# Contiguous parameter loads, one store of the conv output, and a new step order in an attention and state-space kernel

## The chip, the cores and the metric

The kernel runs on 1 core of one Trainium2 chip. The metric is device microseconds (us) of one execution. Below, the engines carry the names of the profile: PE (TensorE), DVE (VectorE), ACT (ScalarE), POOL (GpSimd), SP (SyncE). SP, ACT and POOL also issue DMA transfers, each to queues of its own.

Each run has a state: a run over 1.5% above the fastest of the same kernel counts as slow.

## The reference, cut to what matters

Two independent parts, whose results are concatenated. The change touches only part B, the state-space convolution of 640 channels with 192 states each, over 2048 positions.

```python
# Part A: attention in 32 heads of 20 over 8 keys, each 2 apart; x is 2048x640
qkv = x @ wqkv;  logits = q . k[pos - 2*w], w = 0..7;  o = softmax(logits) . v;  a = o @ wo

# Part B
dt    = exp(log_dt)[:, None]                     # 640 values, bf16
logdA = dt * (A_re + 1j*A_im);  dB = dt * (B_re + 1j*B_im);  Cc = C_re + 1j*C_im   # 640x192 each
K     = einsum("dn,dnl,dn->dl", Cc, exp(logdA*l), dB).real
y     = irfft(rfft(u, 2L) * rfft(K, 2L))[:L] + u * Dskip
return concatenate([a, y], -1)
```

## The kernel before: the parts that matter

The kernel records 1,785 steps and executes them in an explicit list `ORDER`. That list fixes the program order of every engine: a step that waits holds back everything behind it on its engine.

Part B starts with a chain. Six parameters and `log_dt` are loaded (tiles `nat`, `ldt`). They are then "flipped": PE multiplies them with an identity, or with a diagonal of dt, so that the states come to stand on partitions (`ps_tr` in PSUM). From the flips come `ta` and `wi` (log-magnitude and phase per step), from those the tables of sines and magnitudes, and from the flipped B and C the generator `Gt`. Only then can the tables be multiplied into the kernel K (`ps_k`), and only after K come the transforms, the inverse and the output.

```python
# log_dt: channel d = 160g + 32c + t goes to partition 32g + t, column c
def ld_dt():
    for g in range(4):
        ACTE.dma_start(out=ldt()[32*g:32*g+32, :], in_=lsrc[g])
# parameters: the same layout, so rows of 192 bf16 = 384 B
def ld_nat(a):                       # a: A_re, A_im, C_re, C_im, B_re, B_im
    src = (...)[a].rearrange("(g c t) n -> g t c n", g=4, c=NCH, t=32)
    for g in range(4):
        (SP, ACTE, PQ)[min(a, 2)].dma_start(out=nt()[32*g:32*g+32, h], in_=src[g])
# x: four transposing loads on SP
for q in range(4):
    SP.dma_start(out=xT()[:, :, 512*q:512*q+512], in_=A_x[0, 512*q:512*q+512, :], transpose=True)

# u: 8 stages of 4 loads (rows of 160 bf16 = 320 B), regrouped by a DVE copy, written back to DRAM
def ld_u(us=us, s=s):
    for g in range(4):
        PQ.dma_start(out=us()[32*g:32*g+32], in_=usrc[g, :, s])

# inverse(i): i//4 = 0 does chunks 0,1,2 and i//4 = 1 chunks 3,4, for position block q = i%4
for o in range(0, 16, per):
    ...                                                   # matmuls into ps
    if n == 3: ACTE.copy(out=ysb()[:, o:o+per], in_=ps()[:])
    else:      V.tensor_tensor(out=ud()[:, o:o+per], in0=ps()[:], in1=ud()[:, o:o+per], op=A.add)
if n == 3:     V.tensor_tensor(out=ud()[:], in0=ud()[:], in1=ysb()[:], op=A.add)
def store(h):                                             # 192-B rows (3 chunks) or 128-B rows (2 chunks)
    for g in (2*h, 2*h+1):
        (PQ if h else SP).dma_start(out=dst_b[g, :, s, 32*cs[0]:32*cs[-1]+32], in_=ud()[32*g:32*g+32]...)
```

The softmax here doesn't subtract the row's maximum and nothing guards it: scores larger than these inputs give would overflow.

## Time and profile before

| | before |
|---|---|
| time, median of 3 runs | 404.41 us (402.19 to 408.61) |
| span of the profiled run | 406.0 us |
| busy: DVE, PE, ACT | 77%, 74%, 70% |
| DVE busy in the first 50 us | 12.5 us |
| last DVE instruction ends | 398.6 us, 7.4 us before the span does |

The page of the kernel before, its busy times, the DVE and DMA rows (tenths of 40 equal slices of the span) and the count of DMA packets:

```profile
span 406.0 us, 14847 instructions
PE 300.9 (74%) x6407; PEld 198.6 (49%) x6420; DVE 312.5 (77%) x472; ACT 284.0 (70%) x610; POOL 90.1 (22%) x165
DVE  1041499895199997899999977999967986864992
DMA  8999987873458496994611847820345348989766
DMA packets 67325, 72.55 MB, mean 179 GB/s; under 512 B 31140, under 2 KB 57748, under 8 KB 66492
```

No engine is full on average. The DVE row shows where it is not: the first five slices (50 us) are at 0 to 4 tenths, while the DMA row is at 8 or 9. The table of stretches gives it in us. The columns are the stretch, its length, the busy time of each engine, the granted clock, the DMA share (the time of all packets over 16 engines; it can pass 1, as here) and GB/s:

```profile
0.00:50.00 50.00, 21.46 (x139) 10.95 (x142) 12.50 (x30) 19.36 (x55) 17.91 (x37) 1.00 1.14 146
50.00:100.00 50.00, 37.13 (x266) 16.29 (x270) 45.60 (x91) 46.89 (x95) 22.39 (x32) 0.90 0.73 212
```

DVE (third engine column) goes from 12.50 to 45.60 of 50 us. What does it wait for? The timeline of DVE before gives start, length and, in brackets, the idle time ahead of an instruction and who ended it:

```profile
20.62 0.69 DVE L378 TENSOR_SCALAR wk<-ps_tr 128x512 f32<-128x512 f32 x1 [10.60 <-PE ps_tr L359]
...
45.91 0.69 DVE L394 TENSOR_TENSOR pr<-ps_tr,cc 128x512 f32<-128x512 f32 x1 [10.79 <-PE ps_tr L359]
```

Both waits are for flips. PE's timeline says what the flips waited for:

```profile
19.49 0.26 PE L359 MATMUL ps_tr<-dg,nat 128*128 128x64 bf16 x2 [7.96 <-DMA nat<-in_B_A_im_dram]
...
42.63 2.32 PE L555 MATMUL ps_p<-xT,w 128*128 128x512 bf16 x5 [8.84 <-DMA xT<-in_A_x_dram]
44.74 0.31 PE L359 MATMUL ps_tr<-dg,nat 128*128 128x64 bf16 x2
```

The first flip (19.49) waited for A_im. The DMA records, which give the times of every packet, say what A_im waited for. The 640 two-byte pieces of `log_dt` ahead of it on ACT's queue were all done by 4.7 us. Of A_im's own 640 rows half were done by 5.3 us, but the last only at 18.6 us, and from 6.5 us on x's transposed packets were in flight beside them. B_im was late: POOL's timeline has the load behind it waiting for B_im until 38.45.

```profile
38.45 0.58 POOL L571 DMA_DIRECT2D us<-in_B_u_dram  x1 [11.72 <-DMA nat<-in_B_B_im_dram]
```

x's four transposing loads took 41.42 us to issue, as SP's timeline shows:

```profile
4.71 41.42 SPq L302 DMA_TRANSPOSE xT<-in_A_x_dram  x4
```

One more wait comes near the end. In the chain of waits (start, length, what) before, 15 us go to the load that feeds the inverse:

```profile
341.89 15.06 DMA zq<-Zdram
```

### The profile page before, as it was taken

What the parts mean: (1) busy time and instruction counts of PE and PEld (TensorE: products, weight loads), DVE (VectorE), ACT (ScalarE), POOL (GpSimd) and SP (SyncE); (2) the same over time, 40 slices, a digit from 0 to 9 for tenths busy, and PEclk for the clock granted to TensorE, in tenths of its full rate; (3) what the DMA queues carried; (4) which work ended last, traced back from release to release, by engine and by line L of the source; (5) the groups of instructions that cost most, each with busy time, mean ns of one, the idle gap of its engine ahead of it and who ended that gap; (6) DMA issues with size and microseconds to landing.
All of it is one profiled execution on the core that took longest, in us unless ns stands there. A gap on an engine that the chain in (4) does not pass through costs nothing. (4 is left out here: it accounts for less than half of the span.)

```text
span 406.0 us, 14847 instructions
## 1 busy us (share of the span) xinstructions
PE 300.9 (74%) x6407; PEld 198.6 (49%) x6420; DVE 312.5 (77%) x472; ACT 284.0 (70%) x610; POOL 90.1 (22%) x165
## 2 busy tenths in 40 slices
PE   3263769865997974348799998679947879888884
PEld 1121324323543463036586777459625656575673
DVE  1041499895199997899999977999967986864992
ACT  2371389999999798138989868698614718668952
POOL 8050256720000021404110013200020120222252
PEclk9999989996999975558979989898886989969998
DMA  8999987873458496994611847820345348989766
GB/s 130 119 196 110 177 218 215 256 249 121 133 173 253 167 297 160 262 283 130 157 54 37 281 122 197 251 83 3 123 123 158 108 139 291 384 251 282 199 123 135
DMA packets 67325, 72.55 MB, mean 179 GB/s; under 512 B 31140, under 2 KB 57748, under 8 KB 66492
## 3 DMA queue, kind: packets, MB, share of 16 engines
q1 hardware_dynamic: 57964, 54.41, 50.7%
q0 software_dynamic: 6576, 15.31, 15.4%
q10 hardware_dynamic: 2720, 1.89, 2.1%
q8 instruction: 50, 0.82, 0.8%
q14 instruction: 15, 0.12, 0.1%
HBM read 43.98 MB, written 24.98 MB: 170 GB/s over the span
## 5 line engine op out<-in xcount | busy, mean ns | idle before, releaser
L555 PE MATMUL ps_p<-xT,w 128*128 128x512 bf16 x287 | 75.6, 408 | 30.3 <-ACT st L558 16.9
L555 PEld LDWEIGHTS <-w 128*128 128x128 bf16 x300 | 29.6, 103 | 70.4 <-issue 28.3
L529 PE MATMUL ps_k<-Ytab,Xtab 128*20 128x33 bf16 (+1 forms) x2560 | 52.7, 246 | 12.6 <-issue 5.9
L529 PEld LDWEIGHTS <-Xtab 128*20 128x20 bf16 (+1 forms) x2560 | 44.9, 127 | 25.9 <-issue 22.2
L776 DVE TENSOR_TENSOR p<-vb,attn 128x2048 bf16<-128x2048 bf16 x40 | 47.6, 1217 | 9.9 <-PE ps_o L781 4.8
L618 ACT CAST A<-ps_f 128x512 bf16<-128x512 f32 x80 | 43.2, 608 | 13.9 <-PE ps_f L613 13.1
L720 DVE TENSOR_TENSOR prod<-qb,kb 128x2048 bf16<-128x2048 bf16 x40 | 47.6, 1218 | 3.9 <-PE ps_l L725 2.6
L769 POOL DMA_DIRECT2D vb<-vd x40 | 22.0, 556 | 122.0 <-DVE p L776 91.8
L672 ACT CAST S<-ps_f 128x512 bf16<-128x512 f32 x80 | 42.2, 621 | 4.5 <-PE ps_f L668 3.3
L558 ACT CAST st<-ps_p 128x512 bf16<-128x512 f32 x60 | 33.7, 585 | 15.9 <-PE ps_p L555 15.5
L668 PE MATMUL ps_f<-A,cT 128*64 128x128 bf16 x640 | 28.3, 222 | 6.2 <-ACT A L618 2.5
L725 PE MATMUL ps_l<-prod,cGs 128*32 128x512 bf16 x160 | 17.7, 454 | 15.9 <-DVE prod L720 15.7
L675 DVE TENSOR_TENSOR Yf<-S 128x1024 bf16<-128x1024 bf16 x40 | 25.7, 683 | 3.5 <-ACT S L672 3.4
L795 PE MATMUL ps_op<-wo,oT 128*128 128x320 bf16 x160 | 28.2, 325 | 0.1
L668 PEld LDWEIGHTS <-cT 128*64 128x64 bf16 x640 | 20.7, 109 | 14.6 <-issue 13.6
L571 POOL DMA_DIRECT2D us<-in_B_u_dram x32 | 20.0, 632 | 24.6 <-DMA nat<-in_B_B_im_dram 11.7
L189 DVE TENSOR_TENSOR krtmp<-Xtab,Xg 128x1536 bf16<-128x1536 bf16 (+2 forms) x30 | 20.5, 685 | 6.3 <-DMA Xg<-Gdram 6.1
L490 ACT ACTIVATE Stab<-ta 128x192 bf16<-128x192 f32 x80 | 23.7, 362 | 0.3 <-DVE Ytab L512 0.2
L695 ACT CAST Z<-ps_ia 128x512 bf16<-128x512 f32 x40 | 21.4, 599 | 3.5 <-PE ps_ia L689 3.3
L613 PE MATMUL ps_f<-cBD,U 128*64 128x128 bf16 x320 | 22.6, 300 | 0.4 <-ACT A L618 0.2
L689 PE MATMUL ps_ia<-cEA,Yf 64*128 64x128 bf16 x640 | 21.5, 221 | 1.3 <-ACT A L618 0.8
L613 PEld LDWEIGHTS <-U 128*64 128x64 bf16 x320 | 20.2, 205 | 3.7 <-issue 2.5
(104 smaller groups left out, 552.0 us busy)
## 6 DMA issues: line engine op xcount, KB each, us to landing
vb<-vd SPq DMA_DIRECT2D x40, 128.5 KB
vb<-vd POOLq DMA_DIRECT2D x40, 128.5 KB, 4.1
Gdram<-cs SPq DMA_DIRECT2D x22, 192.0 KB
HB<-k_HB SPq DMA_DIRECT2D x2, 2048.0 KB
Zdram<-Z SPq DMA_DIRECT2D x3, 1024.0 KB
zq<-Zdram SPq DMA_DIRECT2D x12, 256.0 KB
kb<-kd SPq DMA_DIRECT2D x4, 657.5 KB
us<-in_B_u_dram POOLq DMA_DIRECT2D x32, 80.0 KB, 4.8
```

The source lines that it names most:

```text
L490: st(lambda k=k: ACTE.activation(out=Stab[c]()[:, k - 1], in_=ta()[:, CW * c:CW * c + CW], func=ACT.Exp, scale=float(-16 * k)))
L529: MM(ps()[32 * g:32 * g + 20, i, :], lhsT=X[c]()[rows, part % 2, :, col + t0 + i], rhs=Y[c]()[rows, :, part % 2, col + t0 + i], start=(par ...
L555: MM(ps()[:], lhsT=w()[:, kt, 128 * ct:128 * ct + 128], rhs=xT()[:, kt, 512 * sc:512 * sc + 512], start=(kt == 0), stop=(kt == 4))
L558: st(lambda so=so, sc=sc, ps=ps: ACTE.copy(out=so()[:, sc], in_=ps()[:]))
L613: MM(ps()[64 * r:64 * r + 64, jj], lhsT=src(16 * dd + 4 * jq + jj), rhs=BD1()[:, r, :], start=(jj == 0), stop=True, skip_group_check=True, ...
L618: st(lambda o=o, ps=ps: ACTE.copy(out=A1[c]()[:, :, sig, o:o + 16].rearrange("p k (j g) -> p k j g", g=4), in_=ps()[:].rearrange("p j (k g ...
L668: MM(ps()[64 * dd:64 * dd + 64, kk, r], lhsT=T()[:, k, r, :], rhs=A1[c]()[:, k, :, 64 * dd:64 * dd + 64], start=(kk == 0 and r == 0), stop ...
L672: st(lambda h=h, ps=ps, Sp=Sp: ACTE.copy(out=Sp()[:, :, :, :, 2 * h:2 * h + 2, :].rearrange("p r s j k g -> p (r s) j k g"), in_=ps()[:].r ...
L675: st(lambda b=b, i=i, Sp=Sp: V.tensor_tensor(out=Yf[c]()[:, 2 * i:2 * i + 2, :, 32 * b:32 * b + 32], in0=Sp()[:, :, 1].rearrange("p r j k ...
L720: st(lambda pr=pr, ct=ct, u2=u2: V.tensor_tensor(out=pr()[:], in0=q()[:, ct].unsqueeze(1).to_broadcast([128, 4, PB]), in1=windows(k()[:, c ...
L776: st(lambda p2=p2, u2=u2: V.tensor_tensor(out=p2()[:], in0=v()[:, :, 2 * u2:2 * u2 + PB], in1=attn[b]()[:, u2].unsqueeze(1).to_broadcast([ ...
L795: MM(ps()[:], lhsT=oT[b]()[:, t, 128 * x:128 * x + 128], rhs=wo_sb()[:, t, 320 * eh:320 * eh + 320], start=(t == 0), stop=(t == 4))
```

## The change

The intent: load every parameter as one contiguous run per partition (channel d = 5p + c on partition p, so 1,920 B per partition instead of five rows of 384 B), load u likewise, and let the flips and the evictions from PSUM do the regrouping. Keep the `u*D` tiles until all five chunks have been added, and store each row of 320 B once. Give all steps a new order. The core of the diff, with the `ORDER` list and some regrouping views left out:

```diff
-    def ld_dt():
-        for g in range(4):
-            ACTE.dma_start(out=ldt()[32 * g:32 * g + 32, :], in_=lsrc[g])
-    st(ld_dt)
+    st(lambda: ACTE.dma_start(out=ldt()[:], in_=B_log_dt.rearrange("(p c) -> p c", c=NCH)))
     def ld_nat(a):
-        src = (...)[a].rearrange("(g c t) n -> g t c n", g=4, c=NCH, t=32)
-        for g in range(4):
-            (SP, ACTE, PQ)[min(a, 2)].dma_start(out=nt()[32 * g:32 * g + 32, h], in_=src[g])
+        src = (...)[a].rearrange("(p c) n -> p (c n)", c=NCH)
+        (SP, ACTE, SP, ACTE, SP, ACTE)[a].dma_start(out=nt()[:, h].rearrange("p c n -> p (c n)"), in_=src)
@@ flip: chunk c is now the innermost index of the PSUM tile @@
-        psb = [bank([128, 512], "ps_tr", tag) for _ in range(2)]
+        psb = [bank([128, 3, 32, NCH], "ps_tr", tag) for _ in range(2)]
...
+    def by_k(ap):
+        return ap.rearrange("p (k c t) -> p k c t", k=3, c=NCH)
+    def by_chunk(t, s):
+        return t.rearrange("p (c k t) -> p k c t", c=NCH, k=6)[:, s.start // 160:s.start // 160 + 3]
-        st(lambda s=s, ps=ps: ACTE.copy(out=ta()[:, s], in_=ps()))
+        st(lambda s=s, ps=ps: ACTE.copy(out=by_chunk(ta()[:], s), in_=by_k(ps())))
...
@@ u: two loads of 10,240 B per partition @@
-            for g in range(4):
-                PQ.dma_start(out=us()[32 * g:32 * g + 32], in_=usrc[g, :, s])
+        PQ.dma_start(out=us()[:]..., in_=B_u[0].rearrange("(l1 a h b) ch -> h (l1 a) (b ch)", a=4, h=2, b=8)[h])
@@ inverse: u*D for all chunks ahead; the store after the second add, 8 rows at a time @@
+        def store(o, h):
+            for g in (2 * h, 2 * h + 1):
+                (PQ if h else SP).dma_start(out=dst_b[g, :, 16*q+o:16*q+o+per], in_=ud[q]()[32*g:32*g+32, o:o+per])
...
-        for h in range(2):
-            st(lambda h=h: store(h))
```

## The prediction

> **What bounds the kernel now.** Over the span (406.0 us) no engine is full: VectorE is busy 312.5 us, TensorE 300.9, ScalarE 284.0 (busy table). The table of stretches splits it. In the first 50 us VectorE is busy only 12.5 us, ScalarE 19.4 and TensorE 21.5, while the DMA engines are at their limit (DMA share 0.8 to 1.3). From 60 us on VectorE is busy 15 to 20 of every 20 us, except 100 to 120 us, where ScalarE (19.9) and TensorE (19.3) are full. So: a start bound by loads, then three nearly full engines, VectorE first.
>
> The waits of the start are for loads that this change touches: TensorE waits 8.0 us for A_im, landing at about 19.5 us behind 640 two-byte packets of log_dt on its queue; VectorE waits 10.6 us for that flip and 10.8 us for the B_im flip, which runs only at 44.7 us (timeline). GpSimd, which issues B and u, is stuck 10.1 and 11.7 us behind its own loads. The Trainium skill ("DMA: Bandwidth & Descriptors", Specifications) says transfers under 512 B miss line rate; this trace has 31,140 of 67,325 packets under 512 B.
>
> **What the change does.**
> - Parameters: 24 loads in 384-B rows become 6 with 1,920 B per partition, issued by ScalarE and SyncE ahead of weights and x, none by GpSimd. log_dt: 640 two-byte pieces become 128 of 10 B. Regrouping moves into the flips: 20 matmuls each as before, evictions of the same size (0.5 to 0.7 us), only strided.
> - u: 32 loads of 320-B rows (20.0 us of GpSimd) become 2 with 10 KB per partition; the eight regroup copies (0.81 us each) stay.
> - conv output: 320-B rows once instead of 192 + 128 B: half the packets (16,384 to 8,192), same 32 issues, all after the last chunk. The u*D products become 4 of about 1.5 us instead of 6.3 us in all: nothing.
> - Order: summed from the trace's durations, work per engine stays (VectorE about -2, ScalarE -5 us: four activation-table loads fewer). The z loads of the inverse stage now stand before the 4 MB of HB, not behind; they are 15.06 us of the chain of waits.
>
> **How much lies on the path.** I expect the six parameters to have landed by 10 to 15 us and the generator (G) work to start near 12 to 18 us rather than 46. VectorE had done about 9 us of work by 46 us, so it could gain up to 27 us. ScalarE, saturated from 60 to 120 us, had done 17 us by then and limits the gain to about 20. x (10,240 transposed 256-B packets) is not faster by itself and the first projections still come at 25 to 40 us, but the new order puts 45 ScalarE operations ahead of the first projection eviction, so this should not bind. The inverse stage gives perhaps 5 us (VectorE idles 4.6 us in 340 to 360 us). The tail stays about 7 us: last add, GpSimd's issues of 0.65 us, a landing of about 4 us.
>
> 404.4 - 20 - 5 gives about 379; I say 377 us, range 364 to 391. Chances: faster 0.89, within 2% 0.09, slower 0.02.
>
> **What would show it.** First B_im flip before 20 us; VectorE over 30 us busy in the first 50 us; no wait of TensorE on A_im over 3 us; packets under 512 B down by some 18,000; no 15-us wait for z; VectorE's total within 4 us of 312.
>
> **What would make it wrong.** Parameters still delayed by x's transposes and the 1.3 MB halves of u; projections so late that attention starves the end; strided PSUM evictions much slower; a lower TensorE clock (now 0.89 mean, 0.5 at 160 to 180 us) when work is denser; stores bunched at the end stretching the tail.

## The result

| | before | after |
|---|---|---|
| time, median (all runs) | 405.29 us (402.19 to 408.61, 4 runs) | 385.33 us (383.80 to 389.74, 4 runs) |
| ratio of fast runs, 95% interval | | 0.9519 (0.943 to 0.9609) |
| span profiled, mean granted clock | 406.0 us, 0.887 | 384.3 us, 0.884 |
| DVE busy in the first 50 us | 12.5 us | 34.15 us |
| last DVE instruction ends, then to the end | 398.6 us, 7.4 us | 372.75 us, 11.5 us |

A ratio is the mean time of one kernel's fast runs over that of the other kernel's fast runs of the same rounds, so it is not quite the ratio of the medians quoted beside it. The kernel is faster by 4.8%. A later control of five rounds on another chip (the run after_again, below) gave 386.67 us.

The same lines of the page after:

```profile
span 384.3 us, 14774 instructions
PE 306.9 (80%) x6420; PEld 201.0 (52%) x6420; DVE 313.6 (82%) x468; ACT 277.6 (72%) x606; POOL 62.4 (16%) x119
DVE  2289996949898799999899999899998586389870
DMA  7972084782935374657986452578157579289957
DMA packets 60428, 72.54 MB, mean 189 GB/s; under 512 B 24372, under 2 KB 51364, under 8 KB 59340
```

DVE does the same work (313.6 against 312.5 us) in a shorter span. Its row is full from the fourth slice on. The first and second stretch of 50 us after:

```profile
0.00:50.00 50.00, 32.98 (x165) 16.42 (x166) 34.15 (x83) 34.41 (x89) 3.01 (x9) 0.90 0.61 173
50.00:100.00 50.00, 35.96 (x600) 18.47 (x600) 40.83 (x75) 33.54 (x70) 8.62 (x12) 0.77 0.63 196
```

In the first 50 us DVE has done 21.65 us more than before. In the second stretch it gave back 4.8. The two waits of 10 us have become shorter. DVE's timeline after:

```profile
8.64 0.66 DVE L380 TENSOR_SCALAR wk<-ps_tr 128x480 f32<-128x480 f32 x1 [2.88 <-PE ps_tr L355]
...
19.72 0.66 DVE L380 TENSOR_SCALAR wk<-ps_tr 128x480 f32<-128x480 f32 x1 [7.42 <-PE ps_tr L360]
...
24.52 1.15 DVE L400 TENSOR_TENSOR Gt<-pr 128x960 bf16<-128x960 f32 x1
```

The 7.42 us that are left are of another kind. PE's timeline after shows no wait for a parameter beyond the first and one of 0.91 us. From 4.75 to 23.5 us PE works through the flips almost without a pause, 0.4 us for each group of a 128x32 and two 64x64 matmuls. From some 10 us on the start is bound by PE.

```profile
4.75 0.24 PE L357 MATMUL ps_tr<-cident,nat 128*128 128x32 bf16 x1 [4.75 <-DMA nat<-in_B_C_re_dram]
...
9.50 2.02 PE L355 MATMUL ps_tr<-dg,nat 128*128 128x96 bf16 x10 [0.91 <-DMA nat<-in_B_A_re_dram]
```

The flips of B_im, the last two in PE's new order, start at 20.3 instead of 44.7 us. They now stand ahead of the first projection (23.18 us on PE), so they no longer wait for x. SP's timeline after has x's loads issued in 21.55 us, half of the time before, though x's loads themselves were not changed:

```profile
2.73 21.55 SPq L293 DMA_TRANSPOSE xT<-in_A_x_dram  x4
```

The 15-us wait for `zq` is gone from the chain of waits. Others have come in. The chain after has these transfers and "issue" (time in which the engine waited for nothing that the profile shows):

```profile
2.12 8.37 DMA nat<-in_B_B_re_dram
...
52.84 8.88 DMA Gdram<-cs
72.77 6.67 DMA Gdram<-cs
...
314.06 6.50 DMA K<-Kdram
323.45 3.81 issue
...
354.45 6.96 DMA vb<-vd
```

Its first line says that B_re had landed at 10.5 us (2.12 + 8.37). The later ones cost DVE its pace for a while: it is busy 13.14 us of 60 to 80 (18.52 before) and 9.65 us of 320 to 340 (15.44 before).

So the 21.7 us of the two spans split like this. DVE was 21.65 us of work ahead at 50 us, and its last instruction ends 25.8 us earlier. The tail after that instruction has grown by 4.1 us (25.8 - 4.1 = 21.7).

### The profile page after: what moved, and what is told of

Its sections match the earlier page's. It is cut to its first block, busy times and chain, and to the rows that moved or that the text cites. A ratio compares the mean times of both kernels' runs of the same rounds, so it can differ in the third digit from the quotient of the medians.

```text
span 384.3 us, 14774 instructions
## 1 busy us (share of the span) xinstructions
PE 306.9 (80%) x6420; PEld 201.0 (52%) x6420; DVE 313.6 (82%) x468; ACT 277.6 (72%) x606; POOL 62.4 (16%) x119
## 4 chain that ended last, share of the span: by engine, by line
PE 43%; DVE 16%; ACT 15%; DMA 11%; issue 10%; POOL 2%; SPq 1%; POOLq 0%; DVEq 0%; ACTq 0%
PE ps_k L531 9%; PE ps_p L557 8%; PE ps_f L611 7%; PE ps_op L793 4%; DMA Gdram<-cs 4%; DMA vb<-vd 3%; DVE p L774 3%; PE ps_f L666 3%; PE ps_l L723 2%; DMA nat<-in_B_B_re_dram 2%; ACT S L670 2%; PE ps_ia L687 2%; ACT A L616 2%; ACT Stab L492 2%; DMA K<-Kdram 2%
## 5 line engine op out<-in xcount | busy, mean ns | idle before, releaser
L557 PE MATMUL ps_p<-xT,w 128*128 128x512 bf16 x300 | 82.5, 436 | 22.1 <-ACT st L560 20.4
L557 PEld LDWEIGHTS <-w 128*128 128x128 bf16 x300 | 31.8, 109 | 68.6 <-issue 41.5
L616 ACT CAST A<-ps_f 128x512 bf16<-128x512 f32 x80 | 44.6, 618 | 20.8 <-PE ps_f L611 20.6
L767 POOL DMA_DIRECT2D vb<-vd x40 | 22.5, 567 | 137.5 <-DVE p L774 100.5
L666 PE MATMUL ps_f<-A,cT 128*64 128x128 bf16 x640 | 29.5, 234 | 2.5 <-ACT A L616 1.2
L666 PEld LDWEIGHTS <-cT 128*64 128x64 bf16 x640 | 22.1, 118 | 12.6 <-issue 10.5
L793 PE MATMUL ps_op<-wo,oT 128*128 128x320 bf16 x160 | 26.7, 306 | 0.2 <-issue 0.2
L492 ACT ACTIVATE Stab<-ta 128x192 bf16<-128x192 f32 x80 | 24.9, 370 | 0.0
L611 PE MATMUL ps_f<-cBD,K 128*64 128x128 bf16 x320 | 16.4, 250 | 8.1 <-issue 5.8
L611 PEld LDWEIGHTS <-U 128*64 128x64 bf16 x320 | 20.3, 204 | 4.9 <-issue 4.2
L188 DVE TENSOR_TENSOR Xtab<-Xtab,Xg 128x1536 bf16<-128x1536 bf16 (+2 forms) x30 | 20.6, 686 | 0.2
L687 PEld LDWEIGHTS <-Yf 64*128 64x128 bf16 x640 | 18.5, 94 | 4.3 <-issue 3.5
```

What stands on the lines that cost most here:

```text
L492: st(lambda k=k: ACTE.activation(out=Stab[c]()[:, k - 1], in_=ta()[:, CW * c:CW * c + CW], func=ACT.Exp, scale=float(-16 * k)))
L557: MM(ps()[:], lhsT=w()[:, kt, 128 * ct:128 * ct + 128], rhs=xT()[:, kt, 512 * sc:512 * sc + 512], start=(kt == 0), stop=(kt == 4))
L611: MM(ps()[64 * r:64 * r + 64, jj], lhsT=src(16 * dd + 4 * jq + jj), rhs=BD1()[:, r, :], start=(jj == 0), stop=True, skip_group_check=True, ...
L616: st(lambda o=o, ps=ps: ACTE.copy(out=A1[c]()[:, :, sig, o:o + 16].rearrange("p k (j g) -> p k j g", g=4), in_=ps()[:].rearrange("p j (k g ...
L666: MM(ps()[64 * dd:64 * dd + 64, kk, r], lhsT=T()[:, k, r, :], rhs=A1[c]()[:, k, :, 64 * dd:64 * dd + 64], start=(kk == 0 and r == 0), stop ...
L687: MM(ps[dd]()[:, jj].rearrange("p l r -> p (l r)"), lhsT=Yf[c]()[d, q, 4 * jq + jj, :], rhs=EA()[d, q, :], start=(jj == 0 and q == 0), sto ...
```

## The experiments

Two questions: which part of the change made the start faster, and by what; and what happened to the rest, that is, the order, the single store and u. All experiments gave the reference's results. One I could not build: the new structure under the old order, since the old list has no place for the new steps and my attempts ended in deadlock or ran out of on-chip space. Order and structure of the second half are therefore told apart only by what the experiments below leave over.

### params_only, params_queues, small_rows, u_old: which part carries the gain

Theory 1: fewer and larger packets in the parameter loads are the gain. Theory 2, the rival: it is the move of the loads to the front of the SP and ACT queues. These four ran on one chip with 7 runs of the kernel before (median 409.66 us).

params_only is the kernel before with contiguous loads of parameters and `log_dt` and the new flips, but the old queues, old u, old stores and the old order. (Eight steps that fill the second half of the phase table had to move ahead of their first reader.)

```diff
-            (SP, ACTE, PQ)[min(a, 2)].dma_start(out=nt()[32 * g:32 * g + 32, h], in_=src[g])
+        (SP, ACTE, PQ)[min(a, 2)].dma_start(out=nt()[:, h].rearrange("p c n -> p (c n)"), in_=src)
```

> The kernel before with the contiguous parameter rows and the regrouping flips alone; queues as before (A_re on SyncE, A_im on ScalarE, B and C on GpSimd), order as before but for eight steps (the second half of the phase table must now be ready before the first phase is used). Theory 1 (small rows and the 640 two-byte packets held the start): A_im lands before 9 us instead of 19.5, B_im before 15 us instead of 44.7, VectorE is over 20 us busy in the first 50 us (12.5 before), and the ratio to the kernel before is 0.95 to 0.975, that is 10 to 20 of the 20 us gained. Theory 2 (queues and order made the gain): A_im lands earlier but the ratio stays within 0.985 to 1.01.

Measured: 386.98 us median, ratio 0.9454 (0.9382 to 0.9526). This bundle (contiguous loads, the flips that they need, eight moved steps) has the whole gain of the change, a little more than theory 1 said (0.95 to 0.975). The first stretch of its table:

```profile
0.00:50.00 50.00, 38.62 (x210) 19.70 (x211) 33.91 (x74) 37.96 (x101) 23.38 (x43) 0.97 0.94 233
```

DVE's 33.91 us match the 34.15 of the changed kernel. Its last DVE instruction ends at 376.3 us (22.3 earlier than before), and the tail is 7.6 us, close to the 7.4 before.

params_queues puts these loads on the SP and ACT queues, as the change does.

```diff
-        (SP, ACTE, PQ)[min(a, 2)].dma_start(...)
+        (SP, ACTE, SP, ACTE, SP, ACTE)[a].dma_start(...)
```

> As the run before it, and the six parameter loads issued first, three from SyncE and three from ScalarE, ahead of x and the weights. Theory 1: at most 4 us better than the rows alone, ratio 0.945 to 0.97. Theory 2 (queue and place in the queue decide): clearly better than the rows alone, by over 6 us, and B_im's first flip before 20 us only here.

Measured: 388.69 us, 0.95 (0.9421 to 0.958). Not better than params_only: theory 2 falls.

small_rows is the changed kernel with each parameter loaded in five pieces of 384 B per partition.

```diff
-        (SP, ACTE, ...)[a].dma_start(out=nt()[:, h].rearrange("p c n -> p (c n)"), in_=src)
+        for c in range(NCH):
+            (SP, ACTE, ...)[a].dma_start(out=nt()[:, h, c], in_=src[:, CW * c:CW * c + CW])
```

> The changed kernel with each parameter loaded as five pieces in 384-byte rows on the same queues (30 issues instead of 6, 3840 packets instead of 768), all else as changed. Theory 1 (packet size): parameters land 5 us or more later than in the changed kernel (last first flip at 11 to 15 us there), and the time is 3 to 8 us longer, ratio to the kernel before 0.96 to 0.975. Theory 2 (order and queue): within 2 us of the changed kernel, ratio 0.947 to 0.957.

Measured: 394.62 us, 0.9601 (0.9512 to 0.9691); the last flip starts at 31.0 instead of 22.5 us, and DVE is busy 25.5 us in the first 50. So small rows cost, but not the whole gain: SP and ACT were held up by their own 15 issues each, so that x's transposes began only at 14.30 us, after the parameters.

u_old is the changed kernel with u loaded as before (the 32 loads and their stages put back).

```diff
-    st(lambda: ld_u(0))
...
+            for g in range(4):
+                PQ.dma_start(out=us()[32 * g:32 * g + 32], in_=usrc[g, :, s])
```

> The changed kernel with u loaded as before (32 GpSimd loads in 320-byte rows, small staging tiles, the first two right after the C flips, the others after the copy that frees their tile), order otherwise as changed. Theory 1 (u's rows are off the path): ratio 0.945 to 0.96, as the changed kernel, GpSimd busy about 80 us instead of 62. Theory 2 (u's two big early loads are part of the gain): over 5 us slower than the changed kernel, ratio over 0.965, VectorE waiting for u or for GpSimd in the first 80 us.

Measured: 385.83 us, 0.9409 (0.9343 to 0.9474). The loading of u is worth nothing that these runs show: the 28 us of POOL's busy time that the change saves (90.1 to 62.4) were not on the path.

### po_2b, po_small, po_both: which small packets

params_only removed two kinds of small packets, the 640 two-byte pieces of `log_dt` and the 384-B rows. These three put one or both back into params_only. They ran on one chip (kernel before: 409.29 us).

```diff
 po_2b
-    st(lambda: ACTE.dma_start(out=ldt()[:], in_=B_log_dt.rearrange("(p c) -> p c", c=NCH)))
+        for c in range(NCH):
+            ACTE.dma_start(out=ldt()[:, c:c + 1], in_=B_log_dt.rearrange("(p c) -> p c", c=NCH)[:, c:c + 1])
 po_small
-        (...)[min(a, 2)].dma_start(out=nt()[:, h].rearrange("p c n -> p (c n)"), in_=src)
+        for c in range(NCH):
+            (...)[min(a, 2)].dma_start(out=nt()[:, h, c], in_=src[:, CW * c:CW * c + CW])
 po_both: both
```

> The kernel with the contiguous parameter rows alone (ratio 0.945 to the kernel before), and log_dt loaded again in 640 two-byte pieces ahead of A_im on ScalarE's queue. Theory A (the two-byte pieces delayed A_im and with it the start, as the prediction says): A_im's flip moves from about 12 us to over 15 us and the ratio rises to 0.96 to 0.98. Theory B (the 384-byte rows and what they do to GpSimd's queue and to x's transposes): under 2 us change, ratio 0.935 to 0.955, A_im's flip within 2 us of 12 us.

> The kernel with the contiguous parameter rows alone, and each parameter loaded again in 384-byte pieces (five issues of 128 rows; A_re on SyncE, A_im on ScalarE, B and C on GpSimd as before). Theory B: B_im's flips over 10 us later than there (over 33 us instead of 21 to 26), x's 256-byte transposed packets take over 40 ns on average in the first 40 us (19 to 42 ns there, about 80 before), ratio 0.97 to 1.0. Theory A: ratio 0.94 to 0.955, B_im's flips within 4 us.

> Both of these undone: contiguous layout and regrouping flips kept, packets as small as in the kernel before. If packet size is the whole cause, the time is that of the kernel before: ratio 0.985 to 1.01. If the layout of the loads or the changed steps matter besides (fewer partitions per issue before, 4 issues of 32 partitions each), it stays under 0.97.

| | median us | ratio (95%) | `log_dt` there by | DVE busy in 50 us |
|---|---|---|---|---|
| params_only | 386.98 | 0.9454 (0.9382 to 0.9526) | 2.7 or before | 33.9 |
| po_2b | 404.63 | 0.9887 (0.9779 to 0.9994) | 28.1 | 12.15 |
| po_small | 396.08 | 0.9723 (0.9636 to 0.9811) | 5.7 or before | 29.3 |
| po_both | 394.33 | 0.9681 (0.9605 to 0.9757) | 7.2 or before | 25.3 |

1,280 bytes in two-byte pieces take away about four fifths of the gain in po_2b (0.9887 against 0.9454). But po_both, which has both kinds, is better than po_2b alone. At 0.9681 it falls into the second branch of its expectation (under 0.97): with packets as small as in the kernel before, more than half of the gain is still there. Packet size is not the whole cause. In the timelines of PE the first B_im flip comes at 24.20 us in params_only and at 26.08 us in po_both, against 44.74 before:

```profile
24.20 0.58 PE L351 MATMUL ps_tr<-dg,nat 128*128 128x96 bf16 x5
```

```profile
26.08 0.58 PE L356 MATMUL ps_tr<-dg,nat 128*128 128x96 bf16 x5
```

What keeps it early (five load issues over 128 partitions instead of four over 32, the new flips, or the eight moved steps) no run here tells apart. po_small has the ratio that theory B expected (0.9723), but not its path: its B_im flips come only 1.8 us later than in params_only (25.96), not over 10, and x's transposed packets took 29 ns on average, not over 40. Its later projections wait for x instead. And in po_2b something other than the count of packets decides. The timelines of ACT and SP in po_2b (a run of the slow state; its start is what counts here):

```profile
28.08 1.28 ACT L334 ACT_TABLE_LOAD   x1 [28.08 <-DMA ldt<-in_B_log_dt_dram]
...
1.64 38.66 SPq L299 DMA_TRANSPOSE xT<-in_A_x_dram  x4
...
34.00 0.66 DVE L380 TENSOR_SCALAR wk<-ps_tr 128x480 f32<-128x480 f32 x1 [3.27 <-PE ps_tr L355]
```

In po_2b SP began with x's transposes at 1.64 us, while ACT was still issuing `log_dt` (0.74 to 3.09 us). In po_both SP first had five pieces of A_re to issue, and the transposes began at 4.08. So a new theory, R: it is a race. Small packets that are in flight together with x's transposes starve. Between 3.5 and 11.5 us of po_2b the DMA records show 223 two-byte packets done beside 1,741 transposed packets of 256 B, 7.8 for each; the last two-byte packet ended at 27.3 us (in po_both at 4.6 us, before x's first packet at 5.6). The Trainium skill ("DMA: Bandwidth & Descriptors", Queues, rings and completion order) gives a possible reason: an engine "round-robins between the queue rows it has work for, at *packet* granularity", and drains a packet of typically 9 to 17 descriptors before it switches. A queue with 640 tiny pieces would then get the same turns as one with large work. The trace does not confirm this: equal turns of equal length would give about one for one, not 7.8, and the length of a turn is not in the records. So the mechanism stays open; what the next run tests is only that being in flight together is what costs.

### po_2b_late_x and before_late_x: the race tested by order alone

po_2b_late_x is po_2b, with SP's five loads of constants moved ahead of x's transposes. No packet is added or removed.

```diff
-ORDER: 0 1 2 6 3 9 4 5 14 13 26 ...              (9, 4, 5 ...: 9 is the first transpose of x)
+ORDER: 0 1 2 6 3 19 20 21 22 23 9 4 5 14 13 26 ...
```

> The kernel with contiguous parameter rows and two-byte log_dt (404.6 us, log_dt landed only at 28 us), with one thing changed: SyncE issues its five constant loads before x's transposed loads, so that these start about 2.3 us later (about 4 us instead of 1.6). Theory R (a race: many small packets get through only one per turn once x's transposed packets are in flight): log_dt lands before 8 us, VectorE is over 25 us busy in the first 50 us instead of 12, and the time goes back to 384 to 394 us, ratio 0.94 to 0.965. Theory S (the two-byte pieces are slow in themselves): log_dt still lands after 15 us and the ratio stays over 0.975.

Measured: 391.52 us, 0.9576 (0.9434 to 0.9718), against 0.9887 without the move. The same lines of its profile (slow too, so like po_2b's):

```profile
7.79 1.28 ACT L334 ACT_TABLE_LOAD   x1 [7.79 <-DMA ldt<-in_B_log_dt_dram]
...
7.62 21.76 SPq L299 DMA_TRANSPOSE xT<-in_A_x_dram  x4
...
13.71 0.66 DVE L380 TENSOR_SCALAR wk<-ps_tr 128x480 f32<-128x480 f32 x1 [3.27 <-PE ps_tr L355]
```

The two-byte pieces are all still there. With the transposes starting 6 us later (7.62 instead of 1.64; I had expected 2.3) they have landed by 7.8 us instead of 28.1. DVE is busy 32.1 us in the first 50. Theory R holds for po_2b: not the small packets as such, but small packets together with the transposes, made its start late. It does not follow that `log_dt` was late in the kernel before. There SP first had four issues of A_re, the transposes were issued at 4.71 us, and `log_dt` was done by 4.7. What was in flight together with the transposes there was A_im.

before_late_x is the kernel before with x's transposes issued after all parameter loads and two small stores (of `st`, to `kd` and `vd`); nothing else is changed.

```diff
-ORDER: 0 1 2 6 3 9 4 5 14 13 26 7 12 48 ...
+ORDER: 0 1 2 6 3 4 5 7 8 16 17 18 9 14 13 26 12 48 ...
```

> The kernel before, small rows and all, with only its order of loads changed: x's transposed loads are issued after all parameter loads and after the two halo stores, which wait for GpSimd to have issued B and C. Theory R (what was lost at the start was lost to the transposed loads of x getting in front of the small packets): A_im's flip before 13 us instead of 19.5, the first B_im flip before 25 us instead of 44.7, x's first matmul 5 to 10 us later at most, ratio 0.945 to 0.975. Theory S (the small rows are slow in themselves): B_im's flip after 30 us, ratio over 0.98.

Measured: 399.32 us, 0.9698 (0.948 to 0.9917, from two fast runs of four): about half of the gain, by order alone. A_im's last row is done at 7.7 instead of 18.6 us, and its flip is early (DVE's `wk` at 11.81 instead of 20.62 us). So theory R holds for A_im. But the second half of the start stays late, as PE's timeline shows (slow):

```profile
34.51 0.58 PE L555 MATMUL ps_p<-xT,w 128*128 128x512 bf16 x1 [19.65 <-DMA xT<-in_A_x_dram]
```

In the old order a projection stands ahead of B's flips on PE, so the whole chain now waits for x instead. DVE is busy only 15.7 us in the first 50. The expectation of a large gain was half right. Moving x back is no substitute for contiguous loads, unless the flips are moved as well.

Why is x itself slow in these runs? By the DMA records the median of x's 10,240 transposed packets took 18 ns in each of before, after, before_late_x and params_only. The means differ: 52.6, 20.3, 36.7 and 24.7 ns, by a few long packets (10.8% of them took over 100 ns before, 0.3% after). In the kernel after, POOL had no load in flight from 8.8 us until 31.9 us; in the kernel before its gathers ran from 2.8 to 40.1 us with gaps of at most 2.5 us; in params_only they had gaps of 5.3 and 2.6 us within x's time. This is a correlation in the records. I have not tested it by itself.

### after_again, store_16, store_split: the tail

Where did the tail of 11.5 us come from? T1: it is the number of store issues (32, each 0.57 to 0.65 us on POOL). T2: it is the bytes and rows that the DMA engines still have to write after the last chunk, since all rows now wait for it. These three ran on one chip in 5 rounds (kernel before: 408.84 us). after_again is the changed kernel, unchanged, as the control.

> The changed kernel again, as the control for the two runs beside it: ratio 0.94 to 0.96; last VectorE instruction to end of span 11 to 12 us.

Measured: 386.67 us (381.55 to 388.37), 0.9619 (0.9435 to 0.9802). Few of the kernel before's runs counted as fast in these rounds, so the interval is wide.

store_16 halves the issues: 16 rows at once, after the second add.

```diff
-            for g in (2 * h, 2 * h + 1):
-                (PQ if h else SP).dma_start(out=dst_b[g, :, 16*q+o:16*q+o+per], in_=ud[q]()[32*g:32*g+32, o:o+per])
+            for g in (2 * h, 2 * h + 1) if o else ():
+                (PQ if h else SP).dma_start(out=dst_b[g, :, s], in_=ud[q]()[32*g:32*g+32])
```

> The changed kernel with the conv output stored once per 16 rows instead of per 8: 16 issues instead of 32, each twice as big. Theory T1 (the tail is the issue of 10 GpSimd and 12 SyncE stores at about 0.6 us each after the last add): the tail shrinks from 11.5 us to 7 to 9 us and the time falls by 2.5 to 4.5 us, 0.6 to 1.2 per cent under the control. Theory T2 (the tail is the writing of the bytes): tail stays 11 to 12 us, no gain.

Measured: 387.52 us (380.82 to 389.92). There is no ratio, since all but one of its runs count as slow beside its own fastest. The last DVE instruction ends at 376.2 us (in a slow run), and the tail is 11.6 us. With half of the issues the tail is the same: T1 falls as a matter of their number. SP's time for them did not halve, since each issue took longer (9.17 us for 6, against 7.09 us for 10). That the DMA engines and not SP set the pace is read from their share of busy time, 0.92 to 0.99 in both kernels (stretches of 3 to 4 us) until 7 to 8 us into the tail; no run tests it.

store_split stores as the kernel before does (192-B rows after chunks 0 to 2, 128-B rows after 3 and 4) within the new order.

```diff
-                (PQ if h else SP).dma_start(out=dst_b[g, :, 16*q+o:16*q+o+per], in_=ud[q]()[32*g:32*g+32, o:o+per])
+                (PQ if h else SP).dma_start(out=dst_b[g, :, s, chs], in_=ud[q]()[32*g:32*g+32, :, chs])
...
+                store(1, 0); store(1, 1)        # in the step of the add of chunks 0 to 2
```

> The changed kernel with the conv output stored as in the kernel before, chunks 0 to 2 when their add is done and chunks 3 and 4 after theirs, 16 rows each: 16,384 packets of 192 and 128 bytes instead of 8,192 of 320. If the half number of packets is worth something, 2 us or more slower than the control; if only the bunching of the issues at the end matters, as fast as the control or up to 3 us faster, tail 8 to 11 us.

Measured: 395.56 us (392.48 to 397.69), 0.9892 (0.9777 to 1.0007). This is the first branch of the expectation (2 us or more slower), and far beyond it: 8.9 us slower than the control beside it, and the runs of the two do not overlap. DVE's timeline, the last lines of store_split and then of the changed kernel:

```profile
374.15 2.56 DVE L863 TENSOR_TENSOR ud<-ps_ib,ud 128x512 bf16<-128x512 f32 x4 [0.32 <-PE ps_ib L856]
376.74 0.96 DVE L868 TENSOR_TENSOR ud<-ud,ysb 128x1536 bf16<-128x1536 bf16 x1
```

```profile
369.20 2.56 DVE L863 TENSOR_TENSOR ud<-ps_ib,ud 128x512 bf16<-128x512 f32 x4 [0.32 <-PE ps_ib L856]
371.79 0.96 DVE L867 TENSOR_TENSOR ud<-ud,ysb 128x1536 bf16<-128x1536 bf16 x1
```

In both kernels the very last DVE step is the add of chunks 0 to 2: under the new order these finish last, next to the others. So a split store can write only a part ahead. Half of the output's 8,192 rows go by SP's queue. When the last DVE instruction had ended, it still had 2,593 of its 4,096 rows of 320 B to write in the changed kernel; with split stores 1,024 rows of 192 B and all 4,096 of 128 B; in the kernel before 2,048 of 128 B. A row took a mean of 23 ns there at 320 B, 15 at 192 B and 13 to 16 at 128 B. The time of all packets that started after that instruction, over 16 engines, against the tail:

| | packets, us | tail, us |
|---|---|---|
| before | 4.5 | 7.4 |
| after | 8.7 | 11.5 |
| store_16 | 8.9 | 11.6 |
| store_split | 10.7 | 13.7 |

The differences agree, and each tail is about 3 us longer than its packets' time, so T2 stands. This covers 2 of the 8.9 us. Why the last DVE instruction comes 5 us later with split stores stays open. In its profile DVE waits 7.80 us for `vb` at 365.1 us, which the changed kernel's does not, and the granted clock was lower too (0.834 against 0.884).

The profile of the changed kernel has several gaps of PE with the label "issue", 9 of at least 1 us (17.8 us in all) against 4 (6.9 us) before. Each of them, in both kernels, falls together with one packet of 16,384 B on the DMA queue that the page calls "instruction", which ended 1.3 to 1.7 us before PE went on. (There are 50 such packets in either run, most of them without a gap.) The 3.81 us in the chain above are one of them. In params_only there are 2 (5.0 us). That PE waits for its own instructions there is argued from this coincidence. No run tests it.

## Why the prediction was right or wrong

The time, 385.33 us, lies in the range of 364 to 391, and 8 us above the centre.

**What bounds the kernel.** Right: a start bound by loads. The contiguous loads with their flips (params_only) give the whole gain, 0.9454. The step "A_im ... behind 640 two-byte packets of log_dt" is not what held A_im: in the kernel before those pieces were done by 4.7 us, and A_im's last row only at 18.6. What the prediction did not see is the race with x's transposes. before_late_x shows it for A_im: with x issued later, and the two-byte pieces still ahead, A_im was done by 7.7 us. That the two-byte pieces can lose this race themselves is shown by po_2b, where x starts earlier than in the kernel before. The Trainium skill's line that the prediction drew on ("DMA: Bandwidth & Descriptors", Specifications: at least 512 B for line rate) agrees in direction: of the parameter rows done before 12 us a 384-B one took 22 ns in the median in the kernel before (27 in the mean), a 1,920-B one 79 in the kernel after, about 17 against 24 B per ns. But this factor of under two is not what cost 20 us: 640 rows at 27 ns are about 1 us on 16 engines.

**"x ... is not faster by itself".** Nothing in x's loads was changed, but they did become faster: their issues went from 41.42 to 21.55 us. And the wait of 10.8 us which the prediction put down to loads "that this change touches" was in part a wait for x: B_im's flip stood behind a projection that waited 8.84 us for it. In the changed kernel the new order puts the flips ahead of every projection; in params_only, in the old order, x itself came early enough (first projection at 17.05 us). The prediction named neither. The result was right because all went the same way.

**Size of the start.** Predicted 20 us, measured 21.65 us of DVE lead at 50 us. The reason given for 20 instead of 27, that ScalarE is full from 60 to 120 us, is not what the trace after shows: ACT is busy 43.5 of these 60 us (58.9 before). So the close match is partly luck. "VectorE over 30 us busy in the first 50 us" (34.15), "no wait of TensorE on A_im over 3 us" (none) and "VectorE's total within 4 us of 312" (313.6) held. "First B_im flip before 20 us" missed narrowly, at 20.3: the flips had become bound by PE itself, and B_im's stand last.

**"The inverse stage gives perhaps 5 us".** The 15-us wait for z is gone, as predicted. DVE's lead at its last instruction is 25.8 us, 4.2 more than at 50 us. So the sum of the two terms, 25, was met by 25.8. That is luck in part. The lead was not kept on the way: it stood at 17.5 us at 340, after the new waits for `Gdram` and `K`, and 8.3 us came after that instead of the 5 predicted. And params_only, whose chain still has a wait of 6.81 us for `zq`, has a lead of 22.3 us at its last DVE instruction.

**"The tail stays about 7 us".** This is the mis-sized term: 11.5 us. The prediction counted half the packets and the same issues, and noted "all after the last chunk" without costing it. After the last DVE instruction the DMA engines had 8.7 us of packets left instead of 4.5. "Stores bunched at the end stretching the tail" stood among the risks. This term of 4.1 us is most of the distance between the sum (379) and the result (385.3). The other 2 us are no more than the spread of runs: the spans of the two profiles differ by 21.7 us, the medians by 19 to 20.

**Packets under 512 B "down by some 18,000".** Wrong: down by 6,768. The count took every 384-B and 320-B row for a packet, but POOL's short rows stand in the records gathered, as packets of 3,840 B and more.

**What the parts are worth.** The new order, u and the store together are worth nothing beyond params_only that these runs can show: 0.9454 (0.9382 to 0.9526) stands beside 0.9519 (0.943 to 0.9609) and 0.9619 (0.9435 to 0.9802). Within the new order the single store is worth about 9 us. So the new order without it is slower than params_only (0.9892, 0.9777 to 1.0007): the new order needs it. Whether the single store is worth anything under the old order, no run shows. u_old has the lowest ratio, 0.9409, but its interval overlaps with the others: no version clearly beats the changed kernel.

**Left open.** How much of the order's new waits (`Gdram`, `K`, "issue") could be won back; whether POOL's gathers are what slows x's transposes; and, within params_only, what the layout of the load issues, the flips and the moved steps are worth beside the packet size (po_both).

## What to carry to other kernels

A few hundred small pieces can hold up a whole kernel, if they must share the DMA engines with a large transposing load: make them contiguous, or issue them some microseconds ahead of it. Look in the DMA records which load was late, not only which one stands first in the queue. Before crediting a bundled change, run its parts alone: here one part was the whole gain, and the others added nothing to it that the runs show. Merging stores saves DMA time per row, but what it saves is paid at the end if the merged row has to wait for the last result; cost the tail by the rows that are still to be written then, times the time per row, over the number of DMA engines.

## What the Trainium skill lacked or had wrong

- "DMA: Bandwidth & Descriptors", Queues, rings and completion order: it states the turn-taking of queues, but no consequence for tiny pieces. Here 640 two-byte pieces landed at 28.1 us beside x's transposes and by 7.8 us ahead of them. From 3.5 to 11.5 us the records show 7.8 transposed packets done for each two-byte one.
- "DMA: Bandwidth & Descriptors", Latency and other measured facts: it gives 261 GB/s for a DMA transpose with a non-contiguous middle dimension. In the kernel after, the best 4 us moved 4,055 packets of 256 B, 260 GB/s, which agrees. In the kernel before, beside other loads, 16 us (7.5 to 23.5) moved 2,426, which is 39 GB/s. No page that I found says how far a transpose falls in company.
- "DMA: Bandwidth & Descriptors", Specifications and Why small descriptors are slow: for trn2 they give a threshold of 512 B and an overhead in cycles, but no measured time of short rows written to DRAM. Here such rows took a mean of 23 ns for 320 B, 15 for 192 B and 13 to 16 for 128 B in the tails.
- "Runtime: NRT & Kernel Launch", Instruction fetch mechanics: it has no figure for a pause of an engine at a block of 16 KiB. Here PE paused for 1.0 to 3.8 us just after packets of 16,384 B on the "instruction" queue, 4 times (6.9 us) in the kernel before and 9 times (17.8 us) after. Only the coincidence is shown.
